# A convolution-attention and feed-forward kernel on one core: blocks 1 and 2 as 64-row tile pairs with w_out stationary, a new order of the work, other spare matmuls

## The chip, the cores and the metric

The kernel runs on one core of one Trainium2 chip. The metric is the device time of one execution in microseconds (us). The engines of the core are TensorE (PE; its weight loads are PEld), VectorE (DVE), ScalarE (ACT), GpSimd (POOL) and SyncE (SP), which issues nearly all transfers. Each works through its own queue of instructions in order; semaphores hold an instruction until what it needs is done.

## The reference, cut to what matters

```python
# x (4, 4096, 192), weight_gen (4, 4096, 8, 7)
w = exp(weight_gen - max over the 7); w = w / (sum over the 7 + 1e-9)
x_pad = 6 zero rows ahead of each sequence of x
attn[b, s, h, g] = sum over k of w[b, s, h, k] * x_pad[b, s + k, h, g]      # 8 heads of 24
h = attn.reshape(16384, 192) @ w_in                                        # (192, 2048)
g = h * (1 / (1 + exp(-1.702 * h)))
out = g @ w_out                                                            # (2048, 192)
```

The weights w_in and w_out come as 64-bit floats; the kernel narrows them itself.

## The kernel before

The 16384 tokens are cut into 32 blocks of 512. For each block POOL and DVE make the softmax and the seven taps, the sum is scaled and split into a high and a low half of 16 bits (three products of halves stand for one fp32 product), SP transposes it by a transfer, and PE multiplies by w_in, ACT and DVE apply the gate and split again, PE multiplies by w_out, and the result is scaled and stored. The hidden width 2048 is cut into 16 units of 128, so a block has 16 units; units are numbered through all blocks (block 1 is units 16 to 31), and two units make a pair (pair 8 is the first of block 1).

Block 0 is computed in fp32, with W and X steps for the first product (192 rows of w_in are 128 rows, W, and 64 rows, X, of which two units share the array) and S steps for the second. Blocks 1 and 2 do the same with 16-bit halves: W is four matmuls of 128 rows (`whole`, lines 569 to 572), X are 64-row pairs (`halves`, 586 and 587), S has the gate's output stationary and w_out moving, 192 columns a matmul (`second`, 628 to 630). From block 3 on (`SWAP = 3`) a P step computes a pair of units by nine steps of two 64-row matmuls (`pair`, 660), an U step the upper 128 output columns of a unit by six 64-row matmuls with w_out stationary (`upper`, 679), and a C step the lower 64 output columns of a block by 48 matmuls on 64 columns each (`lower`, 692). For P, SP also copies x with its two halves of rows exchanged (`xd`, 438) and rows of w_in to the other half (`moved`, 640).

The order on all engines is written out by hand in two tables of names, `ORDER` for the start and `PERIOD`, repeated for two blocks at a time; `act` turns each name into instructions. The names that matter here:

- `s2.0`: the first step of block 2's softmax, a row maximum on DVE over wb (`softmax`, line 205). Blocks 2 and 3 share one transfer of wb, issued by SP ahead of the table (`load_w(1)`, line 196).
- `n1.o0`, `n2.o0` and the like: the narrowing of weights on DVE (508, 511). `ta`, `tb`, `tr`, `ka`, `kb`: taps of block 0, and their transposition through PE.
- `gt.n` and `gm.n`: the gate of unit n, tanh on ACT (592) and the product on DVE (597). `gh.n` and `gl.n`: its halves (610, 612).
- `W.4` and later units write one of four PSUM banks in turn, so W.4 uses the bank of unit 0 after `gm.0` has read it.
- `x1.2`, `tu1`, `xd1`: the last split of block 1's x on DVE (420), its transposition (426) and the exchanged copy.

```python
def gate(u):
    th[u] = t = gpool.tile([P, N], F32, tag="th", name="th", bufs=2)
    nc.scalar.activation(t, hp[u], AF.Tanh, scale=scale[u[0]][:, 4:5] if u[0] else SIG / 2)
    yield
    ...
    nc.vector.scalar_tensor_tensor(to, th.pop(u), 1.0, hp[u], ALU.add, ALU.mult)
```

Of the kernel before, what the change touches and what calls it, by code (L numbers as in the profile page):

```python
# [9 lines left out]
F16 = mybir.dt.float16  # L10
# [17 lines left out]
a4p.2 tu.1 gt.13 gt.12 xd.1 gl.11 P.7 s3.3 stLb.-1 gm.13 U.8 a5.2 gh.13 U.11 gm.12 gl.13 gh.12 U.13 gt.15 gt.14
gl.12 P.8 gm.15 gm.14 gh.15 gl.15 gh.14 U.7 gt.16 U.12 co.0 s4.3 gl.14 a5p.2 U.9 gt.17 U.14 U.15 gm.16 gh.16
gm.17 gh.17 stU.0 gl.16 gl.17 stV.0 P.9 a6.2 gt.19 gt.18 a6p.2 gm.18 U.16 c0.2 P.10 gt.21 gh.18 C.0 gm.19 s5.3  # L30
gt.20 gm.21 gh.21 gm.20 gl.18 gh.19 gl.19 c2.2 s6.3 lp.5 gh.20 gl.20 a0.3 P.11 gl.21 x0.2 x1.2 a1.3 U.20 gt.22
P.12 gm.22 U.21 gt.23 gm.23 gh.22 x2.2 gl.22 a1p.3 gh.23 U.17 gl.23 U.19 gt.25 gt.24 P.13 U.23 gm.24 cg.2 gm.25
gh.24 a2.3 gl.24 a2p.3 gh.25 gt.27 gl.25 U.18 gm.27 P.14 gt.26 U.22 U.24 gh.27 gm.26 tu.2 gh.26 s0.4 gl.27 gt.29
gl.26 stLa.0 gm.29 gt.28 xd.2 P.15 gm.28 gh.29 a3.3 a3p.3 U.25 gh.28 gl.29 gl.28 gt.30 gm.30 gt.31
"""
ORDER = """
ident s0.0 s0.1 s0.2 s0.3 s0.4 s0.5 s0.6 s0.7 warm.15 tb.0 ta.4 nm.i0 tr.4 nb.t0 ta.6 ta.3 ta.0 tr.6 tb.1 tb.1p
ta.5 tb.3 ta.2 tr.3 tb.2 s1.0 tb.3p trb.0 tr.5 ta.1 s1.1 tb.5 nm.t0 tb.4 nb.i0 sum.0.1 tr.2 tr.0 tb.5p n1.i0
n2.i0 s1.2 s1.3 s1.4 ka.1 tb.6 n1.t0 s1.5 n2.t0 nb.i1 trb.2 ka.0 tb.6p W.0 trb.4 nm.i1 kb.3 kb.1 kb.2 n1.i1 W.2
nm.o0 kb.0 W.1 s1.6 a1.0 X.0 n2.i1 nb.o0w n1.o0 gt.0 a1.1 a1.1p gm.0 W.3 n2.o0 W.4 gt.1 nm.o1 gt.2 n1.o1 S.0a  # L40
S.0b a1.2 gm.1 n2.o1 nb.t1 nm.i2 gm.2 gt.3 a1.2p gm.3 W.5 nb.i2w n1.i2 s2.0 n2.i2 nm.i3 s2.1 n1.i3 a1.3 X.1 gt.5
gt.4 gm.5 gm.4 s3.0 W.6 nb.o2w a1.3p s3.1 n2.i3 nm.t1 n1.t1 W.7 W.9 n2.t1 nb.o4w a1.4 nm.o2 gt.6 S.2 n1.o2 S.1b
s2.2 a1.4p nm.o4 W.8 gm.6 n2.o2 n1.o4 na.i2w n2.o4 gt.7 na.i0w a1.5 a1.5p nm.o3 gm.7 na.t0w n1.o3 s2.3 S.3 s2.4
n2.o3 na.o2w S.6 s2.5 S.7 bin.0 X.2 s2.6 bin.1 W.10 gt.9 nm.o5 gm.9 bin.2 s3.2 gt.8 na.o0w S.5 gm.8 ph.t0w a1.6
a1.6p W.11 s3.3 gt.10 a2.0 s3.4 n1.o5 a2.1 gt.11 W.13 n2.o5 lp2 S.4 S.1a c1.0 c1.1 ph.i2w gm.11 gm.10 na.o4w
c1.2 W.12 X.3 s3.5 bout.0 x1.0 S.11 W.14 ph.i0w gt.12 gt.13 bout.1 x1.1 a2.1p a2.2 gm.12 x1.2 a2.2p pd.t0w a2.3
gm.13 W.15 cg1 gt.15 bout.2 gt.14 ph.o0w S.10 S.9 ph.o4w tu1 ph.o2w gm.15 pl.i0w pl.t0w ps.o0w xd1 gm.14 S.8
# [938 lines left out]
```

## Time and profile before

| what | value |
|---|---|
| runs | 1039.88, 1039.54, 1039.30 us (median 1039.54) |
| profiled execution | 1039.64 us, span 1037.9 us |
| PE busy | 1031.1 us, 99% of the span |
| DVE busy | 859.1 us, 83% |
| ACT busy | 715.1 us, 69% |
| POOL busy | 736.2 us, 71% |
| transfers | 70.81 MB, mean 68 GB/s |

The span runs from the first to the last instruction; the rest of the time lies around it. A busy time counts from the start to the end of instructions; PE's matmuls overlap, so PE can be busy all the time and still not be at its peak.

### The profile page before, as it was taken

The numbers are of one execution on the slowest core, as the hardware profiler recorded it, in microseconds if no ns is written. First come the engines' busy times: TensorE is split into PE (matmuls) and PEld (weight loads), VectorE is DVE, ScalarE is ACT, GpSimd is POOL, SyncE is SP. The second block draws the span as 40 slices with busy tenths as digits, with TensorE's granted clock in tenths as the row PEclk, the third lists the DMA queues.
The fourth block names the chain that finished last, engine by engine and source line by source line (L and its number), as shares of the span: only waits on it lengthen the run. The fifth ranks groups of instructions, "written<-read, shape, count | busy, mean of one in ns | idle before, by whom it ended". The sixth has DMA issues, their size and how long they took to land.

```text
span 1037.9 us, 23035 instructions
## 1 busy us (share of the span) xinstructions
PE 1031.1 (99%) x9238; PEld 523.9 (50%) x9238; DVE 859.1 (83%) x1577; ACT 715.1 (69%) x1210; POOL 736.2 (71%) x502
## 2 busy tenths in 40 slices
PE   8999999999999999999999999999999999999998
PEld 6677644454444444445644444444754444444444
DVE  8897888888788787887888788788887879888775
ACT  5876677667677676766767677676766767676674
POOL 8989686957788767786776778767887676876300
PEclk9999999999999999999999999999999999999999
DMA  9303213131221303113131222213113032111110
GB/s 351 107 26 96 57 41 103 32 100 41 80 66 47 103 17 108 37 47 103 27 99 47 55 85 52 89 32 103 43 47 104 16 109 47 37 42 35 44 33 21
DMA packets 70948, 70.81 MB, mean 68 GB/s; under 512 B 52092, under 2 KB 57596, under 8 KB 69432
## 3 DMA queue, kind: packets, MB, share of 16 engines
q1 hardware_dynamic: 70696, 69.20, 23.9%
q8 instruction: 72, 1.18, 0.5%
q14 instruction: 36, 0.29, 0.1%
q10 hardware_dynamic: 144, 0.13, 0.0%
HBM read 31.96 MB, written 12.58 MB: 43 GB/s over the span
## 4 chain that ended last, share of the span: by engine, by line
PE 97%; DVE 1%; DMA 1%; ACT 0%; SPq 0%; issue 0%; ACTq 0%
PE h L660 43%; PE o L679 29%; PE o L692 15%; PE o L625 2%; PE h L564 1%; PE o L628 1%; PE o L630 1%; PE o L629 1%; PE h L580 1%; PE h L569 1%; DMA wb<-in_weight_gen_dram 1%; PE h L572 1%; PE h L571 1%; PE h L570 1%; PE h L586 0%; DVE xs L420 0%
## 5 line engine op out<-in xcount | busy, mean ns | idle before, releaser
L597 DVE SCALAR_TENSOR_TENSOR h<-th,h 128x512 f32<-128x512 f32 x496 | 330.3, 690 | 106.1 <-ACT th L592 105.5
L592 ACT ACTIVATE th<-h,s 128x512 f32<-128x512 f32 x496 | 320.1, 684 | 134.7 <-PE h L660 114.9
L257 POOL TENSOR_TENSOR acc<-acc,prod 128x768 f32<-128x768 f32 x186 | 346.2, 1861 | 14.3
L241 POOL TENSOR_TENSOR prod<-xb,wb 128x768 f32<-128x768 f32 x186 | 293.2, 1576 | 10.6
L660 PE MATMUL h<-xt,w0h 64*128 64x512 f16 x928 | 178.3, 376 | 0.0
L660 PE MATMUL h<-xt,th 64*128 64x512 f16 x464 | 174.0, 376 | 0.0
L610 ACT ACTIVATE g<-h 128x512 f16<-128x512 f32 x228 | 133.8, 597 | 40.9 <-DVE h L597 38.3
L612 DVE SCALAR_TENSOR_TENSOR g<-g,h 128x512 f16<-128x512 f16 x228 | 150.9, 682 | 6.8 <-ACT g L610 3.5
L660 PE MATMUL h<-xd,rt 64*128 64x512 f16 x720 | 138.3, 376 | 0.0
L225 POOL TENSOR_TENSOR wb<-wb,wr 128x224 f32<-128x224 f32 x31 | 17.9, 576 | 163.4 <-DVE wr L219 158.2
L660 PE MATMUL h<-rt 64*128 64x512 f16 x672 | 129.0, 376 | 0.0
L610 ACT ACTIVATE ro<-h 128x512 f16<-128x512 f32 x164 | 97.4, 597 | 35.3 <-DVE h L597 34.7
L612 DVE SCALAR_TENSOR_TENSOR ro<-ro,h 128x512 f16<-128x512 f16 x164 | 108.7, 680 | 3.8 <-ACT ro L610 0.8
L660 PEld LDWEIGHTS <-rt 64*128 64x128 f16 x1392 | 71.7, 94 | 75.9
L660 PE MATMUL h<-xd,th 64*128 64x512 f16 x240 | 90.2, 376 | 0.0
L660 PE MATMUL h<-xt,w0l 64*128 64x512 f16 x464 | 89.6, 377 | 0.0
L660 PE MATMUL h<-xt,tl 64*128 64x512 f16 x232 | 87.2, 376 | 0.0
L660 PE MATMUL h<-rt,th 64*128 64x512 f16 x224 | 84.2, 376 | 0.0
L679 PE MATMUL o<-g,wos 64*128 64x512 f16 x392 | 76.0, 376 | 0.1
L679 PE MATMUL o<-g,woh 64*128 64x512 f16 x392 | 76.0, 376 | 0.0
L679 PE MATMUL o<-g,wol 64*128 64x512 f16 x392 | 76.0, 376 | 0.0
L610 ACT ACTIVATE ri<-h 128x512 f16<-128x512 f32 x104 | 61.3, 597 | 20.3 <-DVE h L597 19.4
(165 smaller groups left out, 1908.0 us busy)
## 6 DMA issues: line engine op xcount, KB each, us to landing
xb<-in_x_dram SPq DMA_DIRECT2D x11, 1344.0 KB, 6.3
out_dram<-osb SPq DMA_DIRECT2D x28, 256.0 KB, 2.1
xd<-xt SPq DMA_DIRECT2D x30, 192.0 KB, 2.9
rt<-xt SPq DMA_DIRECT2D x28, 192.0 KB, 2.9
out_dram<-osb SPq DMA_DIRECT2D x30, 128.0 KB, 2.3
wb<-in_weight_gen_dram SPq DMA_DIRECT2D x15, 224.0 KB, 3.1
ro<-in_moe_w_out_dram SPq DMA_DIRECT2D x8, 384.0 KB, 9.6
xb<-in_x_dram SPq DMA_DIRECT2D x4, 768.0 KB, 5.8
```

The costliest lines, as they stand in the source:

```text
L225: eng.tensor_tensor(w, w, r, ALU.mult)
L241: eng.tensor_tensor(to.rearrange("p j (h g) -> p (j h) g", g=G), xv, wv, ALU.mult)
L257: nc.gpsimd.tensor_tensor(acc, acc, t, ALU.add)
L564: nc.tensor.matmul(hp[u], lhsT=w, rhs=x32[0], start=start, stop=stop)
L592: nc.scalar.activation(t, hp[u], AF.Tanh, scale=scale[u[0]][:, 4:5] if u[0] else SIG / 2)
L597: nc.vector.scalar_tensor_tensor(to, th.pop(u), 1.0, hp[u], ALU.add, ALU.mult)
L610: nc.scalar.activation(g[:, 0], hp[u], AF.Copy, scale=2.0**-12)
L612: nc.vector.scalar_tensor_tensor(g[:, 1], g[:, 0], -(2.0**12), hp.pop(u), ALU.mult, ALU.add)
L625: nc.tensor.matmul(o, lhsT=g[:, s], rhs=w, start=a and j % 2 == 0, stop=z, skip_group_check=True)
L660: nc.tensor.matmul(to, lhsT=w, rhs=x, start=i == 0, stop=i == last)
L679: nc.tensor.matmul(po[blk, e], lhsT=w[h, f * D : f * D + P], rhs=g[h, i], start=first and i == 1, stop=w is woh and n == NF - (4 if blk == ...
L692: nc.tensor.matmul(po[blk, 2][h * C1 : (h + 1) * C1], lhsT=w[:, d + P : d + D], rhs=gg[blk, f + h][:, i], start=f == 0 and i == 1, stop=f ...
```

## The change

Blocks 1 and 2 now use P, U and C steps as the later blocks do: `SWAP` is 1, `whole`, `halves` and `second` serve block 0 alone, the copies of w_in's last rows into `th_` are gone, `moved` has its own buffer in place of a part of `raw_t`, and `move` runs in two parts (`mv.0`, `mv.1`) earlier in the table. Every block gets both xd copies. Twelve fp32 warm-up matmuls stay of fifteen, and 28 spare ones of 256 columns, twelve of 64 rows and 128 weight columns and sixteen as 64x64 tiles, are put among them. Both tables are new.

```diff
-    w0h, w0l, th_ = (const.tile([P, DFF], F16, name=n) for n in ("w0h", "w0l", "wth"))
+    w0h, w0l = (const.tile([P, DFF], F16, name=n) for n in ("w0h", "w0l"))
+    moved = const.tile([P, 2, DFF // 2], F16, name="moved")
...
-    SWAP = 3
+    SWAP = 1
...
-        if blk < SWAP:
-            _, x1, _ = chunks(xt[blk])
-            nc.sync.dma_start(xd[blk][C1:P, 0:J], x1[0:C1])
-            return
         for h in (0, C1):
             nc.sync.dma_start(xd[blk][h : h + C1], t[C1 - h : P - h])
...
-        else:
-            n = int(key[1]) * QC
-            for p0 in (0, C1):
-                for h in range(2):
-                    to = slice(h * DFF // 2 + n, h * DFF // 2 + n + (1 + (key[-1] == "w")) * QC)
-                    nc.sync.dma_start(th_[p0 : p0 + C1, to], hi[h * C1 : (h + 1) * C1])
...
-        nc.tensor.matmul(ps, lhsT=w0l[:, s], rhs=x0, start=start, stop=False)
-        nc.tensor.matmul(ps, lhsT=w0h[:, s], rhs=x2, start=False, stop=False)
-        nc.tensor.matmul(ps, lhsT=w0h[:, s], rhs=x0, start=False, stop=False)
-        nc.tensor.matmul(ps, lhsT=th_[:, h], rhs=x1, start=False, stop=stop)
...
-        nc.tensor.matmul(o, lhsT=lo, rhs=wos[:, d], start=a and j % 2 == 0, stop=False, skip_group_check=True)
-        nc.tensor.matmul(o, lhsT=hi, rhs=wol[:, d], start=False, stop=False, skip_group_check=True)
-        nc.tensor.matmul(o, lhsT=hi, rhs=woh[:, d], start=False, stop=z, skip_group_check=True)
...
-    moved = raw_t[:, 0 : DFF // 4].bitcast(F16).rearrange("p (k n) -> p k n", k=2)
-
-    def move():
+    def move(half):
 
         for k, w in enumerate((w0h, w0l)):
-            to, of = (a.rearrange("p (q n) -> p q n", n=2 * P) for a in (moved[:, k], w))
-            of = of.rearrange("p (q e) n -> p e q n", e=2)
+            to = moved[:, k].rearrange("p (q n) -> p q n", n=2 * P)[:, 2 * half : 2 * half + 2]
+            of = w.rearrange("p (q e n) -> p e q n", e=2, n=2 * P)[:, :, 2 * half : 2 * half + 2]
...
-    few = 3 * NF
+    few = SWAP * NF
...
-        for _ in range(n):
+        other = ps_h.tile([P, N], F32, tag="h5", name="warmb")
+        half = w[:, 0:P].bitcast(F16)
+        c = 2 * P
+
+        def rows(to, h, o=slice(0, P)):
+            nc.tensor.matmul(to[o, 0:c], lhsT=half[h, o], rhs=half[h, 0:c], start=True, stop=True)
+
+        two = (slice(0, P // 2), slice(P // 2, P))
+        for i in range(n):
             nc.tensor.matmul(ps[:, 0:cols], lhsT=w[:, 0:P], rhs=w[:, 0:cols], start=True, stop=True)
+            if i == n // 2 - 3:
+                for quarters in (False, True, False, True, False):
+                    for _ in range(2):
+                        for to, h in zip((ps, other), two):
+                            for o in two if quarters else (slice(0, P),):
+                                rows(to, h, o)
...
-S.0b a1.2 gm.1 n2.o1 nb.t1 nm.i2 gm.2 gt.3 a1.2p gm.3 W.5 nb.i2w n1.i2 s2.0 n2.i2 nm.i3 s2.1 n1.i3 a1.3 X.1 gt.5
...
+s1.6 W.1 kb.2 kb.1 a1.0 n1.i1 n2.i1 X.0 W.3 n1.o0 a1.1 gt.0 s2.0 gm.0 n2.o0 nm.o1 gt.1 gm.1 nb.i2w W.4 n1.o1
...
+cg1 bout.1 x1.0 lp2 W.13 x1.1 ph.t0w bout.2 X.3 x1.2 ph.i2w pl.i0w a2.1p ph.o2w W.15 gt.13 tu1 S.6 W.14 S.11
+ps.o2w gt.15 ph.o0w S.8 gm.13 pl.o2w pl.t0w gt.12 s3.5 ph.o4w gm.12 gt.14 S.10 mv.0 xd1 pl.i2w gm.15 P.8 gt.16
+a2.2 gm.14 gt.17 pl.o0w gm.16 gh.16 P.9 gm.17 gt.19 gh.17 gl.16 gt.18 gm.19 gl.17 co1 S.15b gh.19 S.14b S.12
...
+a2.4p gh.20 gh.21 S.15a gl.20 gt.22 gl.21 a2.5 S.14a a2.5p S.13 gm.22 a2.6 gt.23 gm.23 gh.22 s3.6 gh.23 P.12
```

What the table does to DVE's queue, from the narrowing of the second piece of w_in (`n1.i1`, `n2.i1`: m and ri) on; ro is w_out, g the gate's product, wm<-wb the row maximum `s2.0`. Before:

```order
L508 SCALAR_TENSOR_TENSOR m<-m,bits 128x512
L511 SCALAR_TENSOR_TENSOR ri<-ri,m 128x512 [waits DMAHW4_49,DVE_49]
L508 SCALAR_TENSOR_TENSOR m<-m,bits 128x512 [waits Activation_49]
L597 SCALAR_TENSOR_TENSOR g_310<-th,h 128x512 [waits Activation_49]
L511 SCALAR_TENSOR_TENSOR ro<-ro,m 128x512 [waits DMAHW7_49,DMAHW0_49,DVE_49]
L508 SCALAR_TENSOR_TENSOR m<-m,bits 128x512 [waits Activation_49]
L597 SCALAR_TENSOR_TENSOR g_331<-th,h 128x512
L511 SCALAR_TENSOR_TENSOR ro<-ro,m 128x512 [waits DMAHW4_49,DMAHW3_49,DVE_49]
L597 SCALAR_TENSOR_TENSOR g_338<-th,h 128x512 [waits Activation_49]
L597 SCALAR_TENSOR_TENSOR g_343<-th,h 128x512 [waits Activation_49]
L508 SCALAR_TENSOR_TENSOR m<-m,bits 128x512 [waits Activation_49]
L205 TENSOR_REDUCE wm<-wb 128x32 [waits DMAHW2_49]
```

and now:

```order
L499 SCALAR_TENSOR_TENSOR m<-m,bits 128x512
L502 SCALAR_TENSOR_TENSOR ri<-ri,m 128x512 [waits DMAHW4_49,DVE_49]
L499 SCALAR_TENSOR_TENSOR m<-m,bits 128x512 [waits Activation_49]
L204 TENSOR_REDUCE wm<-wb 128x32 [waits DMAHW2_49]
L564 SCALAR_TENSOR_TENSOR g_339<-th,h 128x512 [waits Activation_49]
L502 SCALAR_TENSOR_TENSOR ro<-ro,m 128x512 [waits DMAHW7_49,DMAHW0_49,DVE_49]
L564 SCALAR_TENSOR_TENSOR g_346<-th,h 128x512 [waits Activation_49]
L499 SCALAR_TENSOR_TENSOR m<-m,bits 128x512
L502 SCALAR_TENSOR_TENSOR ro<-ro,m 128x512 [waits DMAHW4_49,DMAHW3_49,DVE_49]
L564 SCALAR_TENSOR_TENSOR g_369<-th,h 128x512 [waits Activation_49]
L564 SCALAR_TENSOR_TENSOR g_375<-th,h 128x512
```

The row maximum, which waits for a transfer, stood behind the four gate products of units 0 to 3 and now stands ahead of the first of them.

PE's queue at the same place, from W.3 on (h<-x,ri is a W, o<-ro,g an S, h<-x,rt an X of block 0). Before:

```order
L564 MATMUL h<-x_108,ri 128x512
L564 MATMUL h<-x_108,ri 128x512 [waits DMAHW4_49,DVE_49]
L625 MATMUL o<-ro,g_310 128x192 [waits DMAHW7_49,DVE_49]
L625 MATMUL o<-ro,g_310 128x192 x3
L564 MATMUL h<-x_108,ri 128x512 [waits DVE_49]
L580 MATMUL h<-x_109,rt 128x512
```

and now:

```order
L547 MATMUL h<-x_108,ri 128x512
L547 MATMUL h<-x_108,ri 128x512 [waits DMAHW4_49,DVE_49]
L591 MATMUL o<-ro,g_339 128x192 [waits DMAHW7_49,DVE_49]
L591 MATMUL o<-ro,g_339 128x192
L547 MATMUL h<-x_108,ri 128x512 [waits DVE_49]
L591 MATMUL o<-ro,g_346 128x192 [waits DMAHW0_49]
L591 MATMUL o<-ro,g_346 128x192
```

The products of units 0 and 1 with w_out are cut in two and stand apart; W.4, the second row, waits for DVE in both.

SP's queue of transfers, from the load of the third pair of blocks to the first copies for block 1. Before:

```order
L183 DMA xb<-in_x_dram 128x2688 [waits DMAHW7_49,DVE_49,Pool_49]
L546 DMA wth<-th 64x1024 [waits DMAHW0_49,Activation_49]
L546 DMA wth<-th 64x1024 [waits DMAHW1_49]
L546 DMA wth<-th 64x1024 [waits DMAHW2_49]
L546 DMA wth<-th 64x1024 [waits DMAHW3_49]
L426 DMA_TRANSPOSE xt<-xs 128x12x128 [waits DMAHW4_49,DVE_49,Activation_49]
L435 DMA xd<-xt 64x4x128 [waits DMAHW5_49,DMAHW4_49]
```

and now:

```order
L182 DMA xb<-in_x_dram 128x2688 [waits DMAHW7_49,DVE_49,Pool_49]
L425 DMA_TRANSPOSE xt<-xs 128x12x128 [waits DMAHW0_49,DVE_49,Activation_49]
L599 DMA moved<-w0h 64x2x256 [waits DMAHW1_49]
L599 DMA moved<-w0h 64x2x256 [waits DMAHW2_49]
L599 DMA moved<-w0l 64x2x256 [waits DMAHW3_49,DVE_49]
L599 DMA moved<-w0l 64x2x256 [waits DMAHW4_49]
L433 DMA xd<-xt 64x1536 [waits DMAHW5_49,DMAHW0_49]
L433 DMA xd<-xt 64x1536 [waits DMAHW6_49]
```

The copies into wth are gone; between the transposition of block 1 and its exchanged copy stand four copies into moved. All that is ahead of these rows is as it was.

## Rows read from the trace of the kernel before

**Rows 1.** The page, parts 1 and 2: busy times, granted clock by slice.

```profile
PE 1031.1 (99%) x9238; PEld 523.9 (50%) x9238; DVE 859.1 (83%) x1577; ACT 715.1 (69%) x1210; POOL 736.2 (71%) x502
...
PEclk9999999999999999999999999999999999999999
```

**Rows 2.** Stretch: length, busy PE, PEld, DVE, ACT, POOL, clock, transfers.

```profile
15.95:100.00 84.05, 83.97 (x506) 56.11 (x507) 72.43 (x141) 64.04 (x107) 75.19 (x50) 1.00 0.36 107
```

**Rows 3.** PE in order of time: start, us, line, tiles, count [idle before].

```profile
0.99 5.85 PE L766 MATMUL warm<-x 128*128 128x128 f32 x30 [0.99 <-POOL x L773]
7.51 2.92 PE L292 MATMUL tr<-ident,tap 128*128 128x128 f32 x24 [0.68 <-DVE tap L276]
...
15.95 1.13 PE L564 MATMUL h<-x,ri 128*128 128x512 f32 x2 [1.29 <-ACT x L400]
...
21.25 1.99 PE L564 MATMUL h<-x,ri 128*128 128x512 f32 x4
...
25.39 0.70 PE L580 MATMUL h<-x,rt 64*128 64x512 f32 x1
```

**Rows 4.** PE in order of time, 84 to 95: 16-bit steps.

```profile
85.25 0.25 PE L628 MATMUL o<-wos,g 128*128 128x192 f16 x1
...
89.21 0.38 PE L569 MATMUL h<-xt,w0l 128*128 128x512 f16 x1
...
91.58 0.26 PE L628 MATMUL o<-wos,g 128*128 128x192 f16 x1
...
92.58 0.38 PE L569 MATMUL h<-xt,w0l 128*128 128x512 f16 x1
...
94.30 0.25 PE L628 MATMUL o<-wos,g 128*128 128x192 f16 x1
```

**Rows 5.** The chain that ended last: start, us, what.

```profile
3.30 7.43 DMA wb<-in_weight_gen_dram
...
23.24 1.36 PE o L625 x8
...
152.05 1.94 PE h L660 x18
153.99 2.59 PE o L679 x24
...
161.11 5.30 PE o L692 x48
166.42 3.99 PE h L660 x36
```

**Rows 6.** Groups by line and form: weight loads, busy us, mean ns.

```profile
L692 PEld LDWEIGHTS <-woh 128*64 128x64 f16 x464 | 26.3, 110 | 23.8
...
L629 PEld LDWEIGHTS <-g 128*128 128x128 f16 x128 | 12.5, 98 | 1.3
```

**Rows 7.** SP in order of time: issues of transfers.

```profile
16.81 0.34 SPq L196 DMA_DIRECT2D wb<-in_weight_gen_dram  x1
...
49.68 1.56 SPq L426 DMA_TRANSPOSE xt<-xs  x1
...
110.12 1.53 SPq L640 DMA_DIRECT2D rt<-w0h  x2
...
113.08 1.19 SPq L438 DMA_DIRECT2D xd<-xt  x2
```

**Rows 8.** DVE in order of time, 20 to 27.

```profile
20.46 0.70 DVE L508 SCALAR_TENSOR_TENSOR m<-m,bits 128x512 int32<-128x512 int32 x1 [0.26 <-ACT bits L491]
21.12 0.69 DVE L597 SCALAR_TENSOR_TENSOR g<-th,h 128x512 f32<-128x512 f32 x1
...
26.46 0.39 DVE L205 TENSOR_REDUCE wm<-wb 128x32 f32<-128x224 f32 x1 [0.24 <-DMA wb<-in_weight_gen_dram]
```

**Rows 9.** The tile wb, 0 to 40 us: its four transfers.

```profile
DMA to landing us min/median/max: 2.1/8.2/9.6
```

**Rows 10.** The page, part 6: KB each, median us to landing.

```profile
xd<-xt SPq DMA_DIRECT2D x30, 192.0 KB, 2.9
```

More of the change, by code (lines that the diff above doesn't have):

```diff
@@ L28 @@
[L28 to L32, printed above, removed]
@@ L43 @@
[L43 to L47, printed above, removed]
@@ L559, in whole @@
     def whole(u, start, stop):
-        blk, f = u
-        if blk == 0:
-            w = narrowed["i"][:, column(f) : column(f) + P]
-            nc.tensor.matmul(hp[u], lhsT=w, rhs=x32[0], start=start, stop=stop)
-            return
-        x0, x1, x2 = chunks(xt[blk])
-        ps = hp[u].rearrange("p (j t) -> p j t", j=J)
-        s, h = (slice(n, n + P) for n in (column(f), column_of_half(f)))
-        nc.tensor.matmul(ps, lhsT=w0l[:, s], rhs=x0, start=start, stop=False)
-        nc.tensor.matmul(ps, lhsT=w0h[:, s], rhs=x2, start=False, stop=False)
-        nc.tensor.matmul(ps, lhsT=w0h[:, s], rhs=x0, start=False, stop=False)
-        nc.tensor.matmul(ps, lhsT=th_[:, h], rhs=x1, start=False, stop=stop)
-    def halves(u, v, last_u, last_v):
-        blk, f = u
-        if blk == 0:
-            w = narrowed["t"][:, f // 2 * P : (f // 2 + 1) * P]
-            nc.tensor.matmul(hp[u], lhsT=w[0:C1], rhs=x32[1][0:C1], start=not last_u, stop=last_u)
-            nc.tensor.matmul(hp[v], lhsT=w[C1:P], rhs=x32[1][C1:P], start=not last_v, stop=last_v)
-            return
-        _, x1, _ = chunks(xt[blk])
-        a, b = (hp[w].rearrange("p (j t) -> p j t", j=J) for w in (u, v))
-        t = slice(f // 2 * P, (f // 2 + 1) * P)
-        nc.tensor.matmul(a, lhsT=tail[1][0:C1, t], rhs=x1[0:C1], start=not last_u, stop=last_u)
-        nc.tensor.matmul(b, lhsT=tail[1][C1:P, t], rhs=xd[blk][C1:P, 0:J], start=not last_v, stop=last_v)
+        f = u[1]
+        nc.tensor.matmul(hp[u], lhsT=narrowed["i"][:, column(f) : column(f) + P], rhs=x32[0], start=start, stop=stop)
+    def halves(u, v, last_u, last_v):
+        w = narrowed["t"][:, u[1] // 2 * P : (u[1] // 2 + 1) * P]
+        nc.tensor.matmul(hp[u], lhsT=w[0:C1], rhs=x32[1][0:C1], start=not last_u, stop=last_u)
+        nc.tensor.matmul(hp[v], lhsT=w[C1:P], rhs=x32[1][C1:P], start=not last_v, stop=last_v)
     def gate(u):
@@ L735, in store_lower, with store @@
         nc.sync.dma_start(out[blk][P * N : D * N].rearrange("(p n) -> p n", n=N), t)
-    def store(blk, i, last=False):
+    def store(blk, i):
         if i == 0:
@@ L742, in store @@
         rows = out[blk].rearrange("(p j d) -> p j d", j=J, d=D)
-        o, s = po[blk, i], scale[blk][:, 5:6] if blk else 0.5
-        if last:
-            j = 2 * i
-            nc.scalar.activation(osb[blk][:, j : j + 2, :], o, AF.Copy, scale=s)
-            nc.scalar.dma_start(rows[:, j : j + 2, :], osb[blk][:, j : j + 2, :])
-            return
+        o, s = po[blk, i], 0.5
         nc.scalar.activation(osb[blk][:, 2 * i : 2 * i + 2, :], o, AF.Copy, scale=s)
@@ L837, in act @@
             elif k[0] == "c":
-                step(k, scales, int(k[1:]), spare if int(k[1:]) < SWAP + 2 else lambda n=int(k[1:]): (ps_h, "h5", True) if n % 2 else (ps_o, "o1", True))
+                step(k, scales, int(k[1:]), spare if int(k[1:]) < 2 else lambda n=int(k[1:]): (ps_h, "h5", n > 4) if n % 2 or n == 4 else (ps_o, "o1", n > 4))
                 if n == "2":
@@ L949, in laid_back @@
     import numpy as np
-    n, t, swap = 512, 32, 3
+    n, t, swap = 512, 32, 1
     to = np.empty((4, 128, t, 192), o.dtype)
```

115 lines of the change are left out of this document (57 added, 58 removed).

## Prediction

> **What bounds the kernel now.** I read the page first, then the stretches, then the tensor engine's order of time, then DVE and the transfers for the first 30 us. The page has PE busy for 99% of the span [rows 1], but matmuls are pipelined, so a busy PE says little; what counts is whether their starts follow each other without a hole. From 15.95 us on, the stretch view finds 83.97 busy of 84.05 us [rows 2], and in the order of time each group starts where the one before hands over [rows 3, 4, 5]: the reader is to see a queue in which PE waits for nobody from the first fp32 product (15.95) to the end, but for small holes. [...] So the time is the start (15.95 us) plus PE's own work plus a short tail, and an edit counts in two ways only: by the PE time that it adds or takes, and by a hole that it opens in PE's queue. DVE is close behind up to 100 us (72.43 of 84.05 us [rows 2]): if DVE stands still there, PE soon does.
>
> The profiled execution took 1039.64 us (span 1037.9); the sum is made against it. The median of the runs, 1039.54, is 0.1 us lower. About 0.2% (2.1 us) is what a measurement of this kernel can tell from no change.
>
> **PE's work in blocks 1 and 2.** First product, per block. Removed: 16 W steps of four 128-row matmuls; eight matmuls last 92.58 to 94.30, so 1.72 us, and 64 take 13.76. Also removed: four X steps; eight matmuls and one X last from 89.21 to 91.58, 2.37 us, so an X costs 0.65, four 2.60 [rows 4]. Added: eight P steps of 18 half-height matmuls at 1.94 us, 15.52 [rows 5]. That is 16.36 against 15.52: 0.84 less, mostly the switches into and out of 64-row tiles that each X paid (0.65 against 0.43 for its two pairs at 0.215). Second product, per block. Removed: 192 matmuls of 192 columns; 48 took 85.25 to 89.21, 3.96 us, so 15.84 [rows 4]. Added: 96 matmuls for the upper rows (24 take 2.59, so 10.36) and 48 for the lower ones (5.30), and 0.11 for the return from 64-column tiles, seen where two P after a C take 3.99 in place of 3.88 [rows 5]: 15.77. Together 0.91 less a block, 1.8 for two. Against it, block 0's last fp32 S steps now stand between 64-row P steps in two places of the table; an X's entry and return cost 0.22, fp32 steps reload more, so I take 0.3 each, 0.6 (bounds 0.4 and 1.0). Sum of this part: **-1.2 us**.
>
> The rows also show a weight load of 64 columns at 110 ns against 98 ns for a full one [rows 6]; it runs beside the matmul before it, whose step is 0.22 us, so I cost it at nothing. [...]
>
> **What goes with it at no cost.** Four copies of w_in's last rows into wth leave SP's queue; of the eight copies into moved, four come ahead of xd of block 1 (costed below) and four behind it, 0.77 us of issue each [rows 7], where only output stores and later loads follow. The new output path gives ACT the same two passes and DVE two more a block, 0.7 us each like its other passes over 512 columns [rows 8]; DVE is free 17% of the span [rows 1], so if that cover were gone it would cost 2.8 us for both blocks. The warm-up drops three fp32 matmuls for 28 short ones; 30 records of it took 5.85 us and PE then waited 0.68 for a tap [rows 3], so it can end later; that lies under the wait of the next part.
>
> **The wait that moves (the largest term).** s2.0, the row maximum of block 2's weights, reads wb of the second pair of blocks. It waits for that transfer, which SP issues at 16.81 [rows 7] as its 19th in both kernels, with the same transfers ahead of it. In the trace of before DVE came to s2.0 late and still waited 0.24 us: it started at 26.46, released by the transfer [rows 8], 9.6 us after the issue, the longest in [rows 9]. In the new order s2.0 stands ahead of gm.0, the first gate product of block 0 (the DVE fences ahead show both). DVE gets there after the same work as before: m of o0 starts at 20.46 and gm.0 followed at 21.12 [rows 8], so about 21.5 with the 0.3 us that I count for the reordered start. There it stands until 26.43. Behind it: gm.0, n2.o0, gm.1 and all of DVE's queue; s2.0 takes 0.39 and gm.0 0.69 [rows 8], so gm.0 is done at 27.5. For gm.0 wait PE's W.4, which writes the PSUM bank that gm.0 reads, and the first S. Before, W.3 started at 21.25 and W.4 at about 22.2 (the last two of the four records) with no hole [rows 3]. Now W.4 starts at 27.5: **+5.3 us**, with PE idle for some 5.0. The rest of the stage then follows at PE's pace: half of S.0 and of S.1 0.68 each (four S matmuls took 1.36 [rows 5]), W.5 0.86 (from the end of that S, 24.60, to just past X.1's start), W.4 as much and 0.1 for starting after a hole: X.1 at 30.7, where it was 25.39 [rows 3]; DVE's next six passes, one every 0.60 to 0.66 [rows 8], end with gm.3 at about 31.3, in time for the second pair of X.1 at 31.7. PE waits for nobody afterwards, so nothing gives this back. A start that is later by up to 4 us would be swallowed by this wait, so the reordered taps and the warm-up cost nothing more. Bounds: the shortest time of such a transfer in the queue's full stretch is the 7.43 us of the second wb [rows 5]; from 16.81 that is 24.24, and the term 3.1. Upper: 26.46 as seen, 5.3. I take 5.3, since the transfers ahead are the same ones.
>
> **Block 1's first P.** It needs xd at once, where W.16 needed only xt. On SP stand, after x1.2: the transposition (1.56 us of issue), four copies into moved (3.06) and the first of two xd (0.6) [rows 7], then 2.9 to the landing [rows 10]: 8.1 us. The table leaves W.15, S.6, W.14, S.11, S.8 and S.10 after x1.2, 2 x 0.86 + 4 x 1.36 = 7.2 us of PE work, and P's first step, 0.2, needs no xd. I take the difference, **+0.7** (bounds 0, if DVE gets to x1.2 ahead of PE, and 2.3, if the low part of w_in that two of the copies wait for comes late).
>
> **Sum.** 1039.64 - 1.2 + 5.3 + 0.7 = 1044.4 us for the profiled execution, 1044.3 for the median.
>
> **Rivals.**
> *The clock falls in the hole.* The longest idle of PE before is 1.29 us (up to 15.95 [rows 3]), and the clock held, so no row shows 5 us. [...] For: nothing else runs on PE in the hole. Against: no row. [...]
> *The transfer lands sooner.* At 24.24 the hole is 2.2 us shorter: 1042.1.
> *The wait decides nothing.* If wb is there when DVE arrives, by 21.5, less than 4.7 us after its issue, only the PE part is left: 1039.54 - 1.2 + 0.7 = 1039.0, not slower. For: the first wb landed 2.1 us after its issue [rows 9]. Against: that one had an empty queue, this one has six transfers of w_out and w_in ahead.
> *Block 1's P waits.* If x1.2, tu1 and moved come 2.3 us behind PE's work, 1045.9.
> *The change does less than it says.* The swap could be undone by the old order elsewhere; but the new queue holds no 192-column f16 matmul in blocks 1 and 2, so this has no chance of its own.
>
> **How the numbers follow.** Forecast as summed 0.40; clock falls 0.30; sooner landing 0.10; block 1's wait 0.06; no wait 0.14, of which 0.03 for a gain over 0.2% (below 1037.5, which needs a gain in PE that no row shows). Slower holds the first four: 0.86; same 0.11; faster 0.03. The forecast is 1044.3. The range reaches from just below the sooner landing, 1041.3, to the fallen clock with half of the rest of block 1's bound, 1047.3; it leaves out the no-wait case and a rest above.
>
> **What would show it.** In the profile after: DVE's reduction of wb starts near 26.4 and is put down to the transfer with an idle of about 5 us; W.4 starts near 27.5; X.1 near 30.7; eight P and the U and C of blocks 1 and 2 at 1.94, 0.65 and 5.3 us; the last 800 us as before. A fallen clock shows as fp32 records of some 0.86 us apart in place of 0.43 after the hole. Wrong: the reduction starts near 21.5 with no wait, or PE has no hole before 30 us, or new holes of more than 1 us stand later.

## The result and the profile after

The kernel after takes **1050.09 us** (median of four executions, 1049.78 to 1051.76), the kernel before beside it 1039.42: a ratio of 1.0105, with an interval of 1.0088 to 1.0123. That is slower by 10.7 us, against 4.8 forecast and a range that ended at 1047.3. The profiled execution took 1050.1 us with a span of 1048.3, 10.4 us more than the span before.

The page of the kernel after: busy time of the engines, then PE's tenths and the granted clock in 40 slices of 26.2 us [rows 1].

```profile
PE 1034.8 (99%) x9292; PEld 496.8 (47%) x9292; DVE 860.6 (82%) x1581; ACT 719.4 (69%) x1210; POOL 733.6 (70%) x502
PE   7999999999999999999999999999999999999998
PEclk9899999999999999999999999999999999999999
```

PE's first slice has fallen from 8 to 7, and in the second slice (26.2 to 52.4 us) the clock shows an 8, where the page of before has 9 in all. Two stretches tell more, as in [rows 2] (columns: the stretch and its length, busy time and count of PE, weight loads, DVE, ACT and POOL, granted clock, DMA share, GB/s):

```profile
15.78:100.00 84.22, 79.03 (x480) 46.07 (x482) 68.67 (x131) 62.29 (x101) 68.79 (x46) 0.96 0.36 101
100.00:1044.80 944.80, 942.67 (x8708) 440.02 (x8704) 777.90 (x1419) 650.77 (x1100) 652.19 (x426) 1.00 0.23 60
```

PE now misses 5.2 us of the first stretch, at a mean clock of 0.96, and 2.1 us behind it; the prediction had some 5.0 in the first, at full clock, and nothing behind it. What it waits for is in the waits view (engine and line, what it waited for, us in total, times, the longest), PE alone, cut to the lines that matter:

```profile
PE h L547 <- DVE g L564: 4.6, 1, 4.6
PE h L619 <- DVE ro L579: 2.1, 3, 1.8
PE h L619 <- DMA xd<-xt: 0.4, 1, 0.4
```

**The first wait** is the moved maximum. DVE in order of time, against [rows 8]:

```profile
21.10 0.70 DVE L499 SCALAR_TENSOR_TENSOR m<-m,bits 128x512 int32<-128x512 int32 x1 [0.49 <-ACT bits L482]
25.92 0.39 DVE L204 TENSOR_REDUCE wm<-wb 128x32 f32<-128x224 f32 x1 [4.12 <-DMA wb<-in_weight_gen_dram]
26.23 0.68 DVE L564 SCALAR_TENSOR_TENSOR g<-th,h 128x512 f32<-128x512 f32 x1
```

DVE reaches s2.0 at 21.8, stands 4.12 us for the transfer, which SP issued at 17.64, and gm.0 follows at 26.23. PE, against [rows 3] (L547 is W, L591 S, L553 and L554 X):

```profile
21.18 1.13 PE L547 MATMUL h<-x,ri 128*128 128x512 f32 x2
26.96 2.08 PE L547 MATMUL h<-x,ri 128*128 128x512 f32 x2 [4.65 <-DVE g L564]
28.82 1.49 PE L591 MATMUL o<-ro,g 128*128 128x192 f32 x4
30.11 1.91 PE L547 MATMUL h<-x,ri 128*128 128x512 f32 x2
31.81 0.89 PE L591 MATMUL o<-ro,g 128*128 128x192 f32 x4
32.64 0.70 PE L553 MATMUL h<-x,rt 64*128 64x512 f32 x1
```

W.4 starts at 26.96. From start to start its two records take 1.86 us, the four of S behind them 1.29 and W.5's two 1.70, where 0.86 and 0.68 are full rate, which comes back at about 31.8. In between the granted clock is 0.50 (columns as in the stretches above):

```profile
26.96:31.80 4.84, 4.84 (x8) 2.79 (x9) 4.81 (x9) 4.06 (x6) 4.76 (x4) 0.50 0.41 93
```

The clock has fallen in the hole (the same view gives 1.00 from 22.31 to 25.0 and 0.50 from 25.2 to 26.95), and X.1 starts at 32.64, not at 25.39.

**The second wait** is new, and far from anything that the prediction looked at. PE, then DVE, then POOL around 239 us:

```profile
239.13 0.38 PE L638 MATMUL o<-ro,woh 64*128 64x512 f16 x2
241.27 0.39 PE L619 MATMUL h<-xt,w0l 64*128 64x512 f16 x1 [1.76 <-DVE ro L579]
```

```profile
233.65 0.34 DVE L218 RECIPROCAL wr<-wm 128x32 f32<-128x32 f32 x1
234.86 4.38 DVE L419 SCALAR_TENSOR_TENSOR xs<-acc,s,xs 128x512 f16<-128x512 f32 x1
```

```profile
234.14 0.57 POOL L224 TENSOR_TENSOR wb<-wb,wr 128x224 f32<-128x224 f32 x1 [25.29 <-DVE wr L218]
234.65 1.05 POOL L186 MEMSET xb<- 1x1152 f32 x1
235.67 1.53 POOL L240 TENSOR_TENSOR acc<-xb,wb 128x768 f32<-128x768 f32 x1
237.17 1.53 POOL L240 TENSOR_TENSOR prod<-xb,wb 128x768 f32<-128x768 f32 x1
238.78 2.14 POOL L256 TENSOR_TENSOR acc<-acc,prod 128x768 f32<-128x768 f32 x1
```

One DVE pass, x7.1 (the low half of block 7's first 128 columns, both inputs in SBUF), took 4.38 us; passes of that shape took 0.75 us at 113.9, 176.1 and 990.0, where POOL was idle. It began 0.7 us after POOL had started on block 8, and ended 0.46 us after the first pause between two POOL operations (238.70 to 238.78). The gates behind it came late, and PE's next P step waited for them. POOL starts there because s8.5, the reciprocal that it waits for (L218), stands near the end of the new ORDER, on DVE 1.2 us ahead of x7.1.

**Where the 10.4 us are**, from PE's start-to-start times against the same steps elsewhere, and from the starts of C steps of the same block in both kernels (the chain view: start, us, what). Before, then after:

```profile
220.82 5.30 PE o L692 x48
254.72 5.30 PE o L692 x48
```

```profile
227.62 5.30 PE o L651 x48
264.38 5.30 PE o L651 x48
```

The first of the two is 6.8 us late. Up to there W.0 came 0.2 earlier; the hole before W.4 (5.24 between two starts in place of 0.43) cost 4.8; the slow records behind it 2.4, and 0.1 for starting after a hole; xd in P.8 (0.75 in place of 0.21) 0.5; two short waits at 186 and 218 us 0.3. That makes 7.9, so PE's own work, and a wait of 0.3 at 204 us that only the kernel before has, gave back some 1.1. The second C step is 9.7 late: the hole at 239 with two short ones behind it (2.6 by their starts) lies between. Then three P steps wait, at 410, 496 and 747 us, with 0.3 between two of their starts; that makes 0.7 in all, and the C step that started at 1006.33 starts at 1016.71, 10.4 late.

### The profile page after: what moved, and what is told of

Same layout as the page of the kernel before. It is cut to its first block, busy times and chain, and to the rows that moved or that the text cites. A ratio compares the mean times of both kernels' runs of the same rounds, so it can differ in the third digit from the quotient of the medians.

```text
span 1048.3 us, 23169 instructions
## 1 busy us (share of the span) xinstructions
PE 1034.8 (99%) x9292; PEld 496.8 (47%) x9292; DVE 860.6 (82%) x1581; ACT 719.4 (69%) x1210; POOL 733.6 (70%) x502
## 4 chain that ended last, share of the span: by engine, by line
PE 93%; DVE 3%; DMA 3%; ACT 1%; issue 0%; SPq 0%; DVEq 0%; ACTq 0%
PE h L619 46%; PE o L638 30%; PE o L651 16%; DMA ro<-in_moe_w_out_dram 1%; PE o L591 1%; DMA xb<-in_x_dram 1%; DMA rt<-in_moe_w_in_dram 1%; DVE xs L419 1%; DVE g L564 0%; PE h L547 0%; DMA xd<-xt 0%; DVE m L499 0%; DVE ro L579 0%; DVE ro L502 0%; DVE tf L340 0%
## 5 line engine op out<-in xcount | busy, mean ns | idle before, releaser
L564 DVE SCALAR_TENSOR_TENSOR h<-th,h 128x512 f32<-128x512 f32 x496 | 323.5, 691 | 111.8 <-ACT th L559 110.9
L619 PE MATMUL h<-xt,w0h 64*128 64x512 f16 x992 | 196.1, 376 | 0.0
L577 ACT ACTIVATE g<-h 128x512 f16<-128x512 f32 x210 | 123.3, 597 | 53.1 <-DVE h L564 52.5
L619 PE MATMUL h<-xd,moved 64*128 64x512 f16 x768 | 151.1, 376 | 0.4 <-DMA xd<-xt 0.4
L579 DVE SCALAR_TENSOR_TENSOR g<-g,h 128x512 f16<-128x512 f16 x210 | 136.3, 681 | 9.9 <-ACT g L577 5.7
L619 PE MATMUL h<-rt,moved 64*128 64x512 f16 x720 | 141.1, 376 | 0.0
L619 PEld LDWEIGHTS <-moved 64*128 64x128 f16 x1488 | 80.7, 94 | 82.0
L619 PE MATMUL h<-xt,w0l 64*128 64x512 f16 x496 | 100.5, 378 | 2.1 <-DVE ro L579 2.1
L206 POOL TENSOR_TENSOR wb<-wb,wm 128x224 f32<-128x224 f32 x31 | 19.9, 642 | 103.3 <-DVE wm L204 103.3
L638 PE MATMUL o<-g,wos 64*128 64x512 f16 x420 | 84.8, 376 | 0.0
L638 PE MATMUL o<-g,woh 64*128 64x512 f16 x420 | 84.8, 376 | 0.0
```

Of the source, the lines that this page charges most:

```text
L206: eng.tensor_tensor(w, w, m.unsqueeze(2).to_broadcast(shape), ALU.subtract)
L577: nc.scalar.activation(g[:, 0], hp[u], AF.Copy, scale=2.0**-12)
L579: nc.vector.scalar_tensor_tensor(g[:, 1], g[:, 0], -(2.0**12), hp.pop(u), ALU.mult, ALU.add)
L619: nc.tensor.matmul(to, lhsT=w, rhs=x, start=i == 0, stop=i == last)
L638: nc.tensor.matmul(po[blk, e], lhsT=w[h, f * D : f * D + P], rhs=g[h, i], start=first and i == 1, stop=w is woh and n == NF - (4 if blk == ...
```

## The experiments

Theory: the moved wait makes the first hole, the clock falls in it, and x7.1's meeting with POOL makes the second. Rivals stand with each run. Ratios are to the kernel before on the same chip; "profiled" is the one execution whose rows are shown.

**1. The maximum put back.**

```diff
-... X.0 W.3 n1.o0 a1.1 gt.0 s2.0 gm.0 n2.o0 ... gm.3 n1.i2 nb.o2w ...
+... X.0 W.3 n1.o0 a1.1 gt.0 gm.0 n2.o0 ... gm.3 n1.i2 s2.0 nb.o2w ...
```

> The change with one step put back: the row maximum of block 2's weights (s2.0) stands behind gm.3 and n1.i2 again, as in the kernel before; nothing else is moved. Theory: the moved wait alone makes the hole before W.4 (4.8 us in the trace of the change) and the slow clock behind it (2.4 us), so W.4 starts near 22.2 us, X.1 near 25.4, the clock reads 1.00 throughout, and the time is 1050.1 - 7.2 = 1042.9 us (1042.3 to 1043.5). Rival 1, the hole costs only its own length and the slow records are the reordered start's: 1050.1 - 4.8 = 1045.3, with records of 0.85 us still there. Rival 2, the reordered gates or a late transfer of w_out would hold W.4 or the first S anyway: a hole of over 1 us stays and the time is above 1045.5.

Measured: 1044.63 us (1043.38 to 1044.69), ratio 1.0046 [1.0031, 1.0061]. In the profiled execution (1043.38) the hole is gone, X.1 starts at 25.25, and the clock is 1.00. PE's waits there:

```profile
PE h L619 <- DVE ro L579: 2.1, 3, 1.8
PE h L619 <- DMA xd<-xt: 0.4, 1, 0.4
PE top L347 <- DVE tf L342: 0.3, 1, 0.3
```

6.7 us of the forecast 7.2 come back there, 5.5 by the medians, and the median lies 1.1 us above the range. Both rivals fall by the rows: no slow record and no hole is left there. What keeps the other three executions 1.2 us above the profiled one stays open: no trace of them exists, and two of them show a granted clock of 1.00 too.

**2. The hole filled with matmuls.**

```diff
-... X.0 W.3 n1.o0 ...
+... X.0 W.3 fill.40 n1.o0 ...
+            elif k == "fill":
+                fill(int(n))
```

> The change with its wait as it is, and 40 spare fp32 matmuls of 128 columns put on PE between W.3 and W.4, so that PE works through most of the hole (40 x 0.112 = 4.5 of 4.8 us). Theory: W.4 still starts near 27.0, but the clock stays at its upper level, the records from there on stand 0.43 us apart instead of 0.85, and 2.4 us come back: 1047.7 us (1047.2 to 1048.2). Rival, the slow records after the hole have another cause (weights read from a tile that a transfer still writes, the other engines): 1050.1 us, records of 0.85 us as before. If the spare matmuls themselves run at half rate they end late and the time is above 1050.

Measured: 1052.96 us, 1.0129 [1.0114, 1.0144]. A miss of my own: each spare fp32 matmul is two records of 0.11 us, so 40 took 9.09 us and held W.4 back to 30.96. The same with 20 (run 5):

> The change with its wait as it is and 20 spare fp32 matmuls between W.3 and W.4. (40 of them left 80 records of 0.112 us, 9.1 us in all, twice what was meant, so that the filler itself held W.4 back to 30.96; 20 should take 4.5 us and end before the wait does.) Theory: W.4 starts where the transfer lets gm.0 go, 26.5 to 27.6, as in the change, but its records follow at 0.43 us, not 0.85, and the time is the change's less the 2.4 us of the slow clock: 1047.7 us (1047.0 to 1048.3). Rival, the slow records have another cause than PE's idling: 1050.1, records of 0.85 us after W.4.

Measured: 1047.45 us (1046.81 to 1048.42), 1.0077 [1.0063, 1.0091]. DVE waits for the transfer as before, and PE reads:

```profile
21.58 4.63 PE L740 MATMUL fill<-x 128*128 128x128 f32 x40
26.72 1.13 PE L547 MATMUL h<-x,ri 128*128 128x512 f32 x2 [0.51 <-DVE g L564]
27.69 0.84 PE L591 MATMUL o<-ro,g 128*128 128x192 f32 x4
```

W.4 starts 0.24 us sooner than in the change, and its records are back at full rate (0.97 us for two, with 0.11 for the start). The profiled execution is 2.7 us shorter than the change's, so 2.4 of the 10.7 are the clock's, without touching the wait. And with 10 (2.2 us of filler):

> The change with its wait as it is and 10 spare fp32 matmuls behind W.3 (2.2 us), so that PE idles 2.1 to 3.2 us instead of 4.8 before W.4. It asks how much idling the clock stands: in the change the idle of 1.8 us at 239 was followed by records at full rate, the 4.8 us before W.4 by records at half rate. If it holds as with 20 matmuls, 1047.5 us, no record of 0.85 us; if it falls as with none, 1050.0; a fall that comes later or is shorter lies between.

Measured: 1048.51 us (1047.22 to 1049.75), 1.0087 [1.0072, 1.0103], between the two:

```profile
26.90 1.13 PE L547 MATMUL h<-x,ri 128*128 128x512 f32 x2 [2.36 <-DVE g L564]
27.87 1.43 PE L591 MATMUL o<-ro,g 128*128 128x192 f32 x4
29.10 1.91 PE L547 MATMUL h<-x,ri 128*128 128x512 f32 x2
```

After 2.36 us of idling W.4 itself runs at full rate, and the clock falls behind it: it reads 1.00 from 26.9 to 27.9 and 0.50 from 27.95 to 31.3. One of the four executions shows 1.00 throughout; it took 1047.22, the time with 20 matmuls, and the other three 1048.39 to 1049.75.

**3. The wait alone, in the kernel before.**

```diff
-... a1.1p gm.0 W.3 ... n1.i2 s2.0 n2.i2 ...
+... a1.1p s2.0 gm.0 W.3 ... n1.i2 n2.i2 ...
```

> The kernel before with the wait alone added: s2.0 moved ahead of gm.0, all else as it was. Theory: DVE stands still until the transfer has landed near 26, W.4 starts near 27.0 instead of 22.2, the clock falls in the hole, and nothing later gives it back: 1039.4 + 4.8 + 2.4 = 1046.6 us (1046.0 to 1047.3). Rival 1, the fall of the clock belongs to the new warm-up: 1044.2 us. Rival 2, the kernel before has slack behind the hole that takes part of it up: below 1043.5.

Measured: 1046.11 us (1045.49 to 1047.36), 1.0065 [1.0050, 1.0080]: 6.6 us for one name in the table. DVE, then PE behind W.3 at 20.93 (L564 is W, L625 S):

```profile
25.31 0.39 DVE L205 TENSOR_REDUCE wm<-wb 128x32 f32<-128x224 f32 x1 [4.48 <-DMA wb<-in_weight_gen_dram]
```

```profile
26.34 1.63 PE L564 MATMUL h<-x,ri 128*128 128x512 f32 x2 [4.28 <-DVE g L597]
27.76 2.70 PE L625 MATMUL o<-ro,g 128*128 128x192 f32 x8
```

Here the clock falls when W.4 has already started (it reads 1.00 to 26.8 and 0.50 from 26.9 to 30.2), and the slow records cost 1.6 us, not 2.4.

**4. x7.1 ahead of the reciprocal.**

```diff
-... c7.2 s8.5 gh.100 P.51 gl.100 x7.0 cg7 stLa.5 U.96
+... c7.2 gh.100 P.51 gl.100 x7.0 x7.1 s8.5 cg7 stLa.5 U.96
```

> The change with two steps exchanged at the end of its table: DVE does x7.1 (the low half of block 7's first 128 columns) ahead of s8.5 (the reciprocal that starts POOL's run of block 8), not behind it. Theory: in the change x7.1 took 4.38 us because POOL started its run 0.7 us ahead of it and held what both share until its first pause; with POOL idle x7.1 takes 0.75 us, PE has no hole near 239 us, and 2.6 us come back: 1047.5 us (1047.0 to 1048.0). Rival, x7.1 is slow there of itself (the loads and stores then running, ACT's half of the same step): it takes over 3 us again, and the time stays within 0.6 us of 1050.1.

Measured: 1046.73 us (1046.24 to 1047.30), 1.0068 [1.0051, 1.0084], 3.4 us less than the change, below the range. By the profiled executions (1047.30 and 1050.10) it is 2.8 less, of which 0.2 lie in the first stage: W.4 came 0.7 later there, but the slow records cost only 1.5.

```profile
234.15 0.75 DVE L419 SCALAR_TENSOR_TENSOR xs<-acc,s,xs 128x512 f16<-128x512 f32 x1 [0.27 <-ACT xs L416]
238.13 2.02 DVE L419 SCALAR_TENSOR_TENSOR xs<-acc,s,xs 128x256 f16<-128x256 f32 x1
```

With POOL idle x7.1 takes 0.75 us. The smaller x7.2 now meets POOL's first two products and takes 2.02 in place of 0.48, for which PE waits 0.4 us.

**6. The wait taken away by an earlier load**, with every engine's order but SP's as in the change.

```diff
+        load_w(1)
         load_out(1)
...
-        load_w(1)
```

> The change with every engine's order as it is, and only the load of wb(1) issued earlier: ahead of the second piece of w_out, some eight microseconds sooner on SP; five later loads come 0.6 us later for it. Theory, the term is the transfer and not the place of the maximum: s2.0 starts by 21.7 us with no wait for the transfer, W.4 by 22.8, the clock reads 1.00, and the time is that of the first run, 1043.4 to 1044.7 us. Rival, what stands in DVE's queue or the loads that now come later hold gm.0 or the first S all the same: a hole of over 1.5 us before W.4 or the first S, and a time above 1045.5.

Measured: 1044.98 us (1043.46 to 1045.95), 1.0051 [1.0037, 1.0065]. All of block 0 starts 0.9 us later (W.0 at 16.70), but DVE goes through s2.0 without a stop, and it stands between the same neighbours as in the change:

```profile
22.05 0.38 DVE L204 TENSOR_REDUCE wm<-wb 128x32 f32<-128x224 f32 x1
22.34 0.68 DVE L564 SCALAR_TENSOR_TENSOR g<-th,h 128x512 f32<-128x512 f32 x1
```

W.3 and W.4 follow each other (four records from 22.10 to 24.04) and the clock holds. The median is 0.3 us above the range; less the later start it would lie in it. So the place in the queue costs nothing once the transfer is there in time: it takes both, the early place and the late load, to make the hole.

**7 and 8. Repairs together.** Both put s2.0 back and split the copies into moved, so that the two of w_in's high part stand ahead of block 1's transposition; 7 takes x7.1 ahead of s8.5 as run 4 does, 8 moves s8.5 up:

```diff
-... gt.13 tu1 S.6 ... S.10 mv.0 xd1 ...
+... gt.13 mvh.0 tu1 S.6 ... S.10 mvl.0 xd1 ...
-... gl.98 gh.99 C.5 ... c7.2 s8.5 gh.100 ...
+... gl.98 s8.5 gh.99 C.5 ... c7.2 gh.100 ...
```

> Three repairs at once on the change: s2.0 back behind n1.i2 (as in the first run), x7.1 ahead of s8.5 (as in the fourth), and the two copies of w_in's high part into moved put on SP ahead of block 1's transposition, so that xd is issued 1.5 us sooner. From the first run (1043.4 in its profiled execution, 1044.6 median): the hole near 233 us goes, of its 2.6 us 0.4 stay as in the fourth run, so -2.2; the wait for xd in P.8 (0.84 us there) goes: 1040.3 us (1039.6 to 1041.2), 0.1% above the kernel before, whose work on PE in blocks 1 and 2 is all but the same. If the two copies ahead of the transposition hold it up themselves (they wait for ACT's w0h), the wait for xd stays and the time is 1041.2.

> As the run before it, but with s8.5 moved the other way: not behind x7.1 but 4 us ahead, to where POOL can start block 8's run long before DVE comes to x7.1. Theory (x7.1 is held from the moment it meets a running POOL operation until POOL's next pause): POOL starts near 223 us in this kernel's time, its back-to-back stretch (memset and two taps) is over when x7.1 starts, and x7.1 then waits for one operation at most: 0.75 to 2.3 us in place of 4.4. The hole of 2.1 us shrinks below 0.6 us and the time is 1040.0 us (1039.3 to 1041.2). Rival, x7.1 is slow whenever POOL works near it, whatever stands where: over 3.5 us again, a hole of about 2 us, and a time above 1041.5.

Measured: 1040.53 us (1039.93 to 1041.43), 1.0012 [1.0003, 1.0021], and 1039.65 us (1039.12 to 1042.10), 1.0004 [0.9995, 1.0013]. The wait for xd is gone in both. Run 8, DVE and POOL:

```profile
222.79 0.35 DVE L218 RECIPROCAL wr<-wm 128x32 f32<-128x32 f32 x1
227.53 0.86 DVE L419 SCALAR_TENSOR_TENSOR xs<-acc,s,xs 128x512 f16<-128x512 f32 x1
```

```profile
226.31 1.53 POOL L240 TENSOR_TENSOR prod<-xb,wb 128x768 f32<-128x768 f32 x1
227.92 2.15 POOL L256 TENSOR_TENSOR acc<-acc,prod 128x768 f32<-128x768 f32 x1
```

x7.1 comes 0.3 us ahead of POOL's pause at 227.9, and is done in 0.86. With both holes away the change stands within 0.1% of the kernel before: run 7 is that much slower, run 8 can't be told from it, and neither beats it.

**9. Two more moves on run 8**: gate 0 ahead of the bits of w_out, S.12 and S.13 ahead of P.8.

```diff
-... X.0 W.3 n1.o0 a1.1 gt.0 gm.0 n2.o0 ... gm.15 P.8 ...
+... X.0 W.3 gt.0 nb.o0w a1.1 gm.0 n1.o0 n2.o0 ... gm.15 S.12 S.13 P.8 ...
```

> The run before (e8: s2.0 back, s8.5 early, two copies into moved ahead of the transposition) with two more moves. First, gate 0 of block 0 (gt.0 on ACT, gm.0 on DVE) ahead of the bits of w_out's first columns, which wait for a transfer: in e8's profiled execution they held gm.0 up and left a hole of 0.9 us before W.4. Second, S.12 and S.13 ahead of P.8, so that two fp32 steps fewer stand between block 1's P steps. Theory: the hole of 0.9 us goes where it was, the executions scatter less, and the median is 1039.0 us (1038.5 to 1039.6), so 0.04% below the kernel before and within what can be measured of it. A version that beat both would have to be below 1038.4. Rival, P.8 1.4 us later makes P.10 wait for its gates: a new hole after 64 us and 1040.0 or more.

Measured: 1041.17 us (1040.68 to 1042.27), 1.0018 [1.0009, 1.0026]: the rival. PE's waits (L620 is P here):

```profile
PE h L620 <- DVE g L579: 0.7, 3, 0.3
PE o L591 <- DVE ro L502: 0.5, 1, 0.5
```

P steps wait for their gates (from 65 us on), and the wait for w_out went from W.4 to the first S.

**10 and 12. The warm-up alone**, added to the kernel before (with the 28 short matmuls behind the name) and taken from run 8.

```diff
-... s0.7 warm.15 tb.0 ...
+... s0.7 warm.12 tb.0 ...
```

> The kernel before with the new warm-up alone (12 fp32 matmuls and 28 short ones in place of 15 fp32 ones, at the same place of PE's queue). Theory: PE waits for the first tap after either, so nothing comes of it: 1039.4 us (1039.1 to 1039.7), W.0 within 0.3 us of 15.95. Rival 1, the short matmuls keep PE less busy and the taps start at the lower clock: W.0 still waits for DVE's last copy, so at most +0.3. Rival 2, they bring the clock up sooner: the taps are done sooner, W.0 at 15.4 to 15.7, and 1039.0.

> e8 (s2.0 back, s8.5 early, two copies ahead of the transposition) with the old warm-up of 15 fp32 matmuls. The other side of the warm-up's test: added to the kernel before it came with +0.06% (interval through no change). Theory: the warm-up decides nothing, because W.0 waits for DVE's copy of the tokens and that for transfers; e8's 1039.65 again, 1039.3 to 1040.0. Rival: the short matmuls cost the 0.6 us that the tenth run's median showed, and 1039.0 us comes out, which is not to be told from the kernel before either.

Measured: 1040.02 us, 1.0006 [0.9997, 1.0015], and 1039.91 us, 1.0005 [0.9996, 1.0014]. Neither median tells the warm-up from nothing, though run 10's lies 0.3 us above its range. In its profiled execution the first tap on DVE started at 7.00, waiting for x's transfer (6.61 in the kernel before, 6.32 in run 3), and W.0 at 16.38. Run 12 shows something else: PE idled 1.92 us before W.0, the granted clock read 0.50 from 15.95 to 19.3, and X.0 started 4.91 us after W.0, in place of 3.48 in run 8. Four of its eleven executions show a clock of 0.998 (1040.16 to 1040.37 us, the others 1039.18 to 1040.19), none of run 8's reads below 0.999. Whether the new warm-up is what holds the clock up there is not shown.

## Why the prediction was wrong

**The wait that moves: right, its size with some luck.** It put s2.0's start at 26.4 and W.4 at 27.5, the term at 5.3; it was 25.92, 26.96 and 4.8. SP issued the load 0.8 us later than taken (17.64, not 16.81), and s2.0 started 8.3 us behind the issue, not 9.6; the two nearly cancel. Runs 1, 3 and 6 show the term from three sides.

**The clock: a rival that came.** It was given 0.30 and 2.2 us; the clock fell, for 2.4 us by the rows and by run 5. The longest idle of PE in the trace before was 1.29 us, and a hole of 5 was forecast: that no row showed a fall spoke neither for nor against one, and yet it was counted against. Behind the hole of 4.65 us the granted clock was 0.50, and W.5's two records stood 0.85 us apart, near the 0.86 that were named for a fallen clock without a row. No run shows the 2.2 us, which the upper end of the range holds: they were the author's estimate from the pace of the warm-up's records [rows 3], and that a lower clock made these slow is not shown, since the profile's clock column reads 1.00 there. In their place the runs showed 2.4 us in the change, and 1.6 and 1.5 behind the holes of 4.28 and 5.43 us in runs 3 and 4.

**"PE waits for nobody afterwards" and "the last 800 us as before": the step that failed.** The order ahead was read where the diff speaks of blocks 1 and 2, and the rest of the table was taken as the same work in the same order. It is another order throughout, and near the end of ORDER it brought s8.5 and x7.1 together. That made PE wait at 239 us, 2.9 us by the C steps, and the three short waits further on made 0.7. Runs 4 and 8, which part the two steps either way, take the hole at 239 away. The prediction's own sign of being wrong, new holes of more than 1 us later, is what came. The trace before held the warning: x-passes of the same shape took 0.74 to 2.27 us there, and the row for x7.1 itself is

```profile
227.79 1.64 DVE L420 SCALAR_TENSOR_TENSOR xs<-acc,s,xs 128x512 f16<-128x512 f32 x1
```

with POOL's run begun at 224.31, 3.5 us ahead; in the change the lead was 0.7. With the 2.2 us for the clock the forecast would have stood at 1046.5; these 3.6 us are what the range, up to 1047.3, still lacked.

**PE's work in blocks 1 and 2: near.** Forecast -1.2. Run 8, which has only one hole of 0.9 us, gives it most cleanly, by summing PE's start-to-start times line by line. W, X and S of 64.7 us went, and P, U and C grew by 63.1; but P holds three short waits there, at 400, 486 and 737 us (0.6), and the U steps of the kernel before hold the one at 204 us (0.3). Without them it is -1.9, against -1.8. The fp32 steps cost 0.7 more, without the hole, against 0.6; and the small sums for the scales (L347), costed at nothing, 0.2, since two of them now stand among 64-row steps. Net -0.9. The three short waits, in run 8 as in the change, fall into "the last 800 us as before". **xd in P.8** was forecast at 0.7 and cost 0.5 in the change, 0.8 in run 1. **The warm-up** at nothing: runs 10 and 12 don't tell it from nothing by their medians.

Put together, with PE's work as run 8 gives it: 1039.6 - 0.9 - 0.2 + 4.8 + 2.4 + 0.1 + 0.5 + 2.9 + 0.7 = 1049.9, and 1050.1 was measured; the short waits at 186 and 218 and the one at 204 in the kernel before cancel.

## What to carry to other kernels

Where a table of order is replaced as a whole, compare each engine's order over all of it, and look for pairs that come close and weren't: a pass with a wide spread of durations in the trace before is a place where neighbours decide (0.74 to 2.27 us here). A step that waits for a transfer belongs behind everything that the busiest engine waits for, or its transfer has to be issued earlier (run 6); moved ahead of the first gate product it cost 6.6 us by itself. Where a forecast opens a hole in PE's queue that is longer than any in the trace, price the return at the lower clock as part of it: here it cost 1.5 to 2.4 us, behind holes of 4.28 to 5.43.

## What the runs showed of the hardware

Two DVE passes of x, with both inputs in SBUF, lasted until 0.46 and 0.20 us behind POOL's first pause, through several POOL operations that followed without one: x7.1 took 4.38 us in the change, through a memset and two products, and x7.2 2.02 us in run 4, through two products; passes of their shapes beside an idle POOL took 0.75 and 0.48 (at 176.1 and 176.8 in the change). It was not so of every pass: one of 256 columns at 303.83 in the change took 0.93 us and ended at 304.76, 0.28 behind the end of the POOL operation that it met, though the next was recorded from 304.44 on, without a pause. The gates, passes of 512 columns with one input in PSUM, took 0.63 to 0.70 us in the change, all 512 of them, whether POOL worked or not. The durations of the x passes in the kernel after (min, median, max in ns; both widths):

```profile
L419 DVE SCALAR_TENSOR_TENSOR xs<-acc,s,xs x62: 472/894/4385, 53.4 to 993.5; 128x512 f16<-128x512 f32 x31, 128x256 f16<-128x256 f32 x31
```

When the pass started decided: x7.1 took 0.75 us ahead of POOL's run (run 4) and 0.86 started 0.3 us ahead of a pause (run 8), in place of 4.38. What the two engines share is not shown. In the change the memset, which reads nothing, may have held x7.1 too: free of it x7.1 would have been done at 235.61, and the first product is recorded as starting at 235.67; a margin of 0.06 us is too little to show it.

The clock fell when the hole was over in run 3, 0.6 us behind W.4's start, and with 10 spare matmuls, 1.05 us behind it. In run 2 (40 matmuls, a mean clock of 0.998) the hole near 241 was as long as in the change, where no slow record followed; there, 1.3 us after PE had come back, eight steps took 0.42 us each in place of 0.21 (244.59 to 248.00), 1.7 us in all:

```profile
243.33 0.39 PE L619 MATMUL h<-xt,w0l 64*128 64x512 f16 x1 [1.75 <-DVE ro L579]
244.59 1.05 PE L619 MATMUL h<-xt,w0h 64*128 64x512 f16 x2
247.15 1.01 PE L638 MATMUL o<-ro,wol 64*128 64x512 f16 x2
```

Two of run 2's four executions show a clock of 0.998, two 1.00. So the price of a hole in PE's queue was not its length alone: holes of 1.75 to 1.92 us came with a fall (here, and before W.0 in run 12) and without (at 239 in the change, before W.0 in run 8), and a hole of 5.43 us lost less to the clock than one of 4.65.
